# Moving the state's products, K's decays and the old state's decay to the front of a step in a linear-attention and feed-forward kernel

## The chip, the cores and the metric

The kernel runs on one core of a Trainium2 chip. The metric is the device time of one execution in microseconds, lower is better. Three runs of the kernel before took 573.32, 575.26 and 572.74 us, median 573.32.

The engines are named as in the profile: PE multiplies matrices (PEld is its weight load), DVE is the vector engine, ACT the scalar engine, POOL the GpSimd engine, and SP issues most DMAs.

## The reference

An attention block with a decaying state (RWKV-6) for 4 batches, 8 heads, 768 tokens and 48 channels a head, followed by a feed-forward block with a gated activation over the 3072 tokens:

```python
def _attn_ref(r, k, v, w, u):
    state = np.zeros((B, H, D, D))
    for t in range(S):
        cur = np.einsum('bhd,bhe->bhde', u[None] * kt, vt)
        y[:, :, t] = np.einsum('bhd,bhde->bhe', rt, state + cur)
        state = wt[:, :, :, None] * state + np.einsum('bhd,bhe->bhde', kt, vt)

def _moe_ref(x, w_in, w_out):                  # (3072, 384) (384, 2048) (2048, 384)
    h = x @ w_in
    sp = np.maximum(h, 0.0) + np.log1p(np.exp(-np.abs(h)))
    return (h * erf(sp)) @ w_out
```

All data is float32.

## The kernel before

**Tiles and steps.** The work is cut into 12 steps (`n_steps`): step s handles 128 tokens of two batches, with all heads, and the two pairs of batches alternate, so step s continues the state that step s - 2 left. A step's 128 tokens are two halves of 64 (`NC = 2`). The attention of a step does this:

- `prepare(s)`, a generator, runs a step ahead, in portions that a `next(following, None)` or a token `F` sends off. For the late steps it has POOL multiply the decays into totals (`tot_sb`, L438), and then DVE and POOL work out the terms inside blocks of 16 tokens side by side: products of r and k with `u` (L565, L568), of k and r within a block (`multiply`, L515 to L525, and `multiply_last`, L534), decays applied to r and k (`fade`, L493), decays combined (L486), and sums over the channels (`sum_up`, L559). It sends k, by now multiplied with its decays inside the block, through DRAM into the layout that the state needs (`kTs[s]`, DMAs L607 and L617), and the sums the same way (L609, L611).
- `level_products` (L671) multiplies r and k for spans of 32 and of 64 tokens; `take_level` puts them into `own`, by a masked copy on DVE (L681) or a copy on ACT (L688).
- `from_own` (L703) multiplies `own` with v into `y`, in two halves, `swap` 1 and 0, with a small copy on DVE between them (`fence`, L712); `through_state` (L729) adds what the old state and the state in the middle of the step (`middle`) give, copies `y` to `xT` and sends some of it on by DMAs. In the late steps the `y` of step s - 1 is made at the front of step s.
- `state_part` (L778) multiplies k with v for both halves. From them come `middle` (old state decayed, plus the first half; L857) and the new state (`middle` decayed, plus the second half; L863). The decays are multiplied in by POOL (L832, L860) into the tile `faded`. K is first multiplied with the decays over blocks (`spread[s]`, L837, on DVE).

The feed-forward block runs beside it on PE: `hidden` (L1153) multiplies `xT` of step s - 1 with `w_in` in eight pieces, each into one of two tiles `m` in PSUM and copied out by ACT (L1162); softplus and erf follow on ACT (L1109, L1113), the gating multiplication on DVE (L1118). `project_fast` (L1275) multiplies the gated result of step s - 3 with `w_out` in seven pieces; sums of blocks (`blend`, L1252 to L1258, on DVE) and copies into lanes of PSUM (`to_lane`, L1233, on ACT) save one of eight products. It takes the two tiles `m` as well: the first is last read by DVE at L1295, the second at L1300, and the first two pieces of `hidden` behind it go into the same two tiles.

**Order.** Every engine works through its instructions in the order in which the code issues them. For steps five to eleven that order is written out in `attend_late`, which calls `run` at seven places (`front`, `near`, 0 to 4); each place has a list of tokens: `P` is a piece of `project_fast`, `H` a piece of `hidden`, `s`, `e` and `m` softplus, erf and gating of a chunk, `k` a copy to a lane, `S` a blend, `F` a portion of `prepare`:

```python
USUAL = (
    "s P", "m", "ey P m s P P ep P", "m k22y P F P k11p F F", "S1", "S2 S3 H k12y S4 H F",
    "s H ey m H H F s H ep H H",
)
```

The products for 32 tokens, for 64 tokens and for the state use the same bank of PSUM, one after the other (`products(..., 0)`); the other bank is a lane. SP's queue has, at place 3, the loads of rows and decays of later steps. In step eleven there are no pieces of `hidden` behind the state's products; the weights are combined there on DVE (L1330), and after it the hidden products of the last two steps are made together.

Of the kernel before, what the change touches and what calls it, by code (L numbers as in the profile page):

```python
# [17 lines left out]
P = 128  # L18
# [3 lines left out]
HC = 64  # L22
NC = 2
# [17 lines left out]
DIRECT = 4  # L41
NEAR_LOG = 4
# [49 lines left out]
def kernel(  # L92
# [14 lines left out]
    nc = tc.nc  # L107
    PSUM = bass.MemoryType.PSUM

    n_steps, _, _, JP, C = rkw.shape  # L110
    NH, D = v.shape[2:]
    NP = JP // NJ
    NE = NH // JP
# [5 lines left out]
    SPC = NB // NJ  # L119
# [20 lines left out]
    middle = const.tile([P, JP, D], FP32, name="middle")  # L140
    faded = [const.tile([P, JP, D], FP32, name="faded")] * NC
# [22 lines left out]
    def products(shape, n=None):  # L164

        if n is None:
            n = turns["next"]
            turns["next"] = 1 - n
        names = "abc"[: len(shape) - 1]
        return banks[n][:].rearrange(  # L170
            f"p ({' '.join(names)}) -> p {' '.join(names)}", **dict(zip(names, shape[1:]))
        )

    loaded = {}
# [8 lines left out]
    def load_w(s):  # L183
        ws[s] = ins.tile([P, JP, C], FP32, name="w")
        nc.sync.dma_start(out=ws[s][:], in_=rkw[s][:, 2])
# [52 lines left out]
    def near_log(s):  # L238
        return NEAR_LOG - (s == DIRECT)
# [97 lines left out]
    def rows(e, n=D):  # L337
        return slice(e * EP, e * EP + n)

    both = slice(0, EP + D)  # L340
# [49 lines left out]
    def prepare(s):  # L390


        in_t = loaded[s][0]
        if s < DIRECT:
            rk1 = att.tile([P, 2, JP, C], FP32, name="rk1", bufs=1)
            ready[s] = (rk1,)
            parts = 1 if s else NJ
            def multiply_u(i, x):
                n = slice(i * JP // parts, (i + 1) * JP // parts)
                with_u, plain = (  # L400
                    [
                        t.rearrange("p n (t two) -> p n t two", two=2)[..., one]
                        for t in (rk1[:, x, n], in_t[:, x, n] if s else turns["first"][:, i, x])
                    ]
                    for one in (x, 1 - x)
                )
                if not s and not (x and not i):
                    nc.vector.tensor_mul(
                        with_u[0], with_u[1],
                        u_sb[:, :, None].to_broadcast([P, NP, C // 2]),  # L410
                    )
                    nc.vector.tensor_copy(out=plain[0], in_=plain[1])
                    return
                for p in range(NP):
                    of = slice(p, None, NP)
                    nc.scalar.mul(
                        out=with_u[0][:, of], in_=with_u[1][:, of], mul=u_sb[:, p : p + 1]
                    )
                nc.scalar.copy(plain[0], plain[1])

            if s < 2:
                for i in range(parts):
                    for x in range(2):
                        multiply_u(i, x)
                return
            yield
            yield
            multiply_u(0, 0)
# [42 lines left out]
        levels = near_log(s)  # L471
# [16 lines left out]
        def fade(engine, x, level):  # L488

            half = 1 << level - 1  # L490
            of = split(totals[level - 1], 1)[1 if x is k else 0][:, :, 0]
            to = split(x, half)[0 if x is k else 1]
            engine.tensor_mul(  # L493
                to, to, of[:, :, None, :].to_broadcast([P, NEAR // 2 // half, half, D])
            )
# [71 lines left out]
        fade(beside, k, 1)  # L567
        nc.vector.tensor_mul(own_terms, own_terms, r)  # L568
        fade(nc.vector, r, 1)
        if levels < NEAR_LOG:  # L570
            yield
        sum_up(1)
        multiply(nc.vector, 2)
# [67 lines left out]
    kTs, spread = {}, {}  # L641

    def parts_of(s):

        c, i = divmod(s, SPC)
        in_t, vt = loaded[s]
        made, tots, tot = ready[s]
        ends = tot.rearrange("p (n h) -> p n h", h=NC)
        return c, in_t, vt, made, states[i][c % 2], states[i][1 - c % 2], ends

    def by_pair(t):

        return lambda x, n: t[:, x, n]
# [40 lines left out]
    def from_own(s, own, swap):  # L694
        vt = loaded[s][1]
        for j in range(NJ):
            for q in range(0, NP, 2):
                for h in range(NC):
                    e = h ^ swap
                    for p in (q, q + 1):  # L700
                        n = j * NP + p
                        t = slice(h * HC, (h + 1) * HC)
                        nc.tensor.matmul(  # L703
                            y[at(e, p), e, p // 2, j, t],
                            lhsT=vt[t, n * NE + e, :], rhs=own[t, e * JP + n, :],
                            start=swap == 1 and not j and not q, stop=True,
                            skip_group_check=True,
                        )

    def fence():  # L710

        nc.vector.tensor_copy(  # L712
            out=seen[:].rearrange("p (e g t) -> p e g t", e=NE, g=NP),
            in_=y[:].rearrange("p e q j t -> p e (q j) t")[..., HC - 1 : HC + 1],
        )
# [53 lines left out]
    def state_part(s, kT, ps, halves=None):  # L769

        vt = loaded[s][1]
        if halves is None:
            halves = range(1 if s >= n_steps - SPC else NC)
        for n in range(JP):
            for h in halves:
                for e in range(NE):
                    t = slice(h * HC, (h + 1) * HC)
                    nc.tensor.matmul(  # L778
                        ps[h][e][rows(e), n, :D],
                        lhsT=kT[t, e * JP + n, :],  # L780
                        rhs=vt[t, n * NE + e, :],
                        start=True,
                        stop=True,
                    )
# [27 lines left out]
    def attend_late(s, run):  # L812

        c, in_t, vt, own, S, S_next, ends = parts_of(s)
        RK = by_pair(in_t)
        before = s - 1 if s - 1 > DIRECT else None
        if before:
            from_own(before, ready[before][0], 1)
            fence()
        pp = products([P, NE, JP, HC], 0)  # L820
        level_products(pp, RK, LOG - 1)
        scale(s, LOG - 1)
        take_level(own, pp, LOG - 1)
        run("front", None)
        if before:
            from_own(before, ready[before][0], 0)
            through_state(before, xTs[before])
            if s + 1 < n_steps:
                load_step(s + 1)
        following = prepare(s + 1) if s + 1 < n_steps else iter(())  # L830
        next(following, None)
        nc.gpsimd.tensor_mul(faded[0][:], S[:], ends[:, :, 0:1].to_broadcast([P, JP, D]))  # L832
        next(following, None)
        run("near", None)
        next(following, None)
        kT = kTs[s]
        nc.vector.tensor_mul(  # L837
            kT[:].rearrange("p (e n) d -> p n e d", e=NE),
            kT[:].rearrange("p (e n) d -> p n e d", e=NE), spread[s][:],
        )  # L840
        run(0, following)

        pp = products([P, NE, JP, HC], 0)
        level_products(pp, RK, LOG)
        if s + 1 < n_steps:
            spread_blocks(s + 1, pp)
        take_level(own, pp, LOG)
        if s > DIRECT + 1:
            scale(s, LOG)
        run(1, following)  # L850
        if s == DIRECT + 1:
            scale(s, LOG)
        ps = products([P, NC, JP, HC], 0)
        ps = [[ps[:, h]] * NE for h in range(NC)]
        state_part(s, kT, ps)
        run(2, following)
        nc.vector.tensor_add(middle[both], faded[0][both], ps[0][0][both, :, :D])  # L857
        run(3, following)
        if s < n_steps - SPC:
            nc.gpsimd.tensor_mul(  # L860
                faded[1][:], middle[:], ends[:, :, 1:2].to_broadcast([P, JP, D])
            )
            nc.vector.tensor_add(S_next[both], faded[1][both], ps[1][0][both, :, :D])  # L863
        run(4, following)

    def attend_first(xT):
# [590 lines left out]
        run_late(s, order[k])  # L1457


    STAGES_LATE = ("front", "near", 0, 1, 2, 3, 4)  # L1460
    LATE = {
        DIRECT + 1: (
# [73 lines left out]
    for kk in range(KT):  # L1536
        n = D // KT
        to, of = (x.rearrange("p (e m) -> p e m", e=NE) for x in (apart[:, kk], ident[:]))
        nc.vector.tensor_copy(out=to[:, :, D:], in_=of[:, :, kk * n : (kk + 1) * n])
    load_first()  # L1540
    with tc.manual_schedule(
# [15 lines left out]
        for s in range(n_steps):  # L1557
# [44 lines left out]
            def run(n, following):  # L1602
                if n == 3 and s < n_steps - 2:
                    load_rows(s + 2)
                if n == 3 and s + 3 < n_steps:
                    load_w(s + 3)
                run_late(s, LATE.get(s, USUAL)[STAGES_LATE.index(n)], following)

# [11 lines left out]
        s = n_steps  # L1620
# [107 lines left out]
```

## Time and profile before

| | |
|---|---|
| median of three runs | 573.32 us (572.74 to 575.26) |
| profiled execution, its own time | 574.36 us |
| its span | 572.6 us |
| PE busy | 564.2 us (99%), 7320 instructions |
| DVE busy | 452.7 us (79%), 506 |
| ACT busy | 358.5 us (63%), 495 |
| POOL busy | 246.8 us (43%), 265 |
| granted clock of PE | 0.999 |
| state products L778 | 205 ns each in the median, 704 records |
| hidden products L1153, 128x256 | 382 ns each, 960 records |

A row of the view by time reads: start, duration, engine, line, operation, tile written and tiles read, shapes, count, and in brackets how long the engine stood idle before and what released it. A matmul of float32 leaves two records and they are pipelined, so the start of the next group says more than a group's own duration. The spans on POOL are rough. In the view by stretches each row gives the length of the stretch and the busy time of each engine in it.

Step seven runs from 276.99 us to 321.29 us, counted from the first `y` product at its front.

### The profile page before, as it was taken

The numbers are of one execution on the slowest core, as the hardware profiler recorded it, in microseconds if no ns is written. First come the engines' busy times: TensorE is split into PE (matmuls) and PEld (weight loads), VectorE is DVE, ScalarE is ACT, GpSimd is POOL, SyncE is SP. The second block draws the span as 40 slices with busy tenths as digits, with TensorE's granted clock in tenths as the row PEclk, the third lists the DMA queues.
The fourth block names the chain that finished last, engine by engine and source line by source line (L and its number), as shares of the span: only waits on it lengthen the run. The fifth ranks groups of instructions, "written<-read, shape, count | busy, mean of one in ns | idle before, by whom it ended". The sixth has DMA issues, their size and how long they took to land.

```text
span 572.6 us, 16719 instructions
## 1 busy us (share of the span) xinstructions
PE 564.2 (99%) x7320; PEld 500.6 (87%) x7320; DVE 452.7 (79%) x506; ACT 358.5 (63%) x495; POOL 246.8 (43%) x265
## 2 busy tenths in 40 slices
PE   8899999999999999999999999999999999999997
PEld 5688887578998998998998998898898899989997
DVE  8774886999899899799699599599599596477730
ACT  3658877645458858747756766766675771489500
POOL 4557380731885884384285185176075000000000
PEclk9999999999999999999999999999999999999999
DMA  7596671440426324245245236234232201000000
GB/s 256 199 297 269 224 224 43 187 158 10 148 64 188 104 63 163 38 158 168 35 145 176 40 121 198 41 112 166 47 112 84 47 9 35 2 2 1 27 29 27
DMA packets 54082, 63.24 MB, mean 110 GB/s; under 512 B 35161, under 2 KB 40569, under 8 KB 52985
## 3 DMA queue, kind: packets, MB, share of 16 engines
q1 hardware_dynamic: 53624, 61.98, 34.4%
q8 instruction: 57, 0.93, 0.7%
q10 hardware_dynamic: 384, 0.20, 0.1%
q14 instruction: 17, 0.13, 0.1%
HBM read 52.39 MB, written 8.69 MB: 107 GB/s over the span
## 4 chain that ended last, share of the span: by engine, by line
PE 89%; DVE 5%; DMA 2%; ACT 1%; POOL 1%; issue 1%; SPq 0%; DVEq 0%; ACTq 0%; POOLq 0%
PE m L1275 33%; PE m L1153 32%; PE c L1378 6%; PE pp L671 5%; PE m L1185 4%; PE y L703 2%; PE y L729 2%; PE pp L778 2%; DVE in L364 1%; DMA words<-in_moe_w_in 1%; PE pp L990 1%; PE pp L1063 1%; DMA u_sb<-in_u 1%; DVE h L1118 1%; POOL tot_sb L386 0%
## 5 line engine op out<-in xcount | busy, mean ns | idle before, releaser
L1153 PE MATMUL m<-xT,w_in_sb 128*128 128x256 f32 x960 | 214.9, 382 | 0.2 <-ACT h L1162 0.2
L1153 PEld LDWEIGHTS m<-xT,w_in_sb 128*128 128x128 f32 x960 | 179.9, 190 | 25.5 <-ACT h L1162 0.6
L364 DVE TENSOR_TENSOR in<-in,tot_sb 128x1024 f32<-128x1024 f32 (+1 forms) x55 | 77.4, 1408 | 5.9 <-PE pp L671 3.4
L1162 ACT COPY h<-m 128x512 f32<-128x512 f32 x80 | 46.3, 580 | 47.8 <-PE m L1153 47.5
L1275 PE MATMUL m<-mixed,h 128*128 128x192 f32 x320 | 56.7, 331 | 0.0
L1275 PE MATMUL m<-w_out_sb,h 128*128 128x192 f32 x320 | 56.2, 329 | 0.0
L1275 PEld LDWEIGHTS m<-mixed,h 128*128 128x128 f32 x320 | 51.8, 190 | 0.9
L1275 PEld LDWEIGHTS m<-w_out_sb,h 128*128 128x128 f32 x320 | 52.0, 190 | 0.5
L1275 PE MATMUL m<-w_out_sb,room 128*128 128x192 f32 x288 | 49.7, 326 | 0.0
L1275 PEld LDWEIGHTS m<-w_out_sb,room 128*128 128x128 f32 x288 | 47.3, 190 | 0.1
L1113 ACT ACT_TABLE_LOAD x28 | 35.9, 1283 | 10.5 <-DVE h L1118 8.4
L534 POOL TENSOR_TENSOR words<-words 128x384 f32<-128x384 f32 x28 | 39.7, 1448 | 0.0
L671 PEld LDWEIGHTS pp<-in 48*48 48x48 f32 (+4 forms) x2368 | 30.1, 120 | 10.9 <-issue 5.8
L493 POOL TENSOR_TENSOR words<-words,own 128x384 f32<-128x384 f32 x21 | 30.1, 1433 | 22.0 <-DVE words L524 13.0
L1109 ACT ACT_TABLE_LOAD x28 | 35.9, 1283 | 1.8 <-issue 1.3
L486 POOL TENSOR_TENSOR own<-rest 128x384 f32<-128x384 f32 x7 | 9.7, 1384 | 61.0 <-ACT o L1281 61.0
L671 PE MATMUL pp<-in 48*48 48x32 f32 (+4 forms) x2368 | 34.0, 206 | 0.3 <-DVE in L364 0.3
L534 POOL TENSOR_TENSOR rk<-words 128x384 f32<-128x384 f32 x28 | 33.4, 1225 | 0.0
L559 DVE TENSOR_REDUCE sums<-rk 128x16 f32<-128x768 f32 (+2 forms) x31 | 31.6, 1021 | 0.0
L438 POOL TENSOR_TENSOR tot_sb<-tot_sb 128x256 f32<-128x256 f32 (+4 forms) x50 | 29.9, 598 | 3.8
L1109 ACT ACTIVATE room<-h 128x1024 f32<-128x1024 f32 x28 | 29.6, 1057 | 0.3
L319 POOL TENSOR_TENSOR w_out_sb<-w_out_sb,rest 128x768 int32<-128x768 int32 x8 | 18.3, 2290 | 21.9 <-DVE w_out_sb L311 21.9
(214 smaller groups left out, 1008.7 us busy)
## 6 DMA issues: line engine op xcount, KB each, us to landing
in<-in_rkw SPq DMA_DIRECT2D x8, 1024.0 KB, 5.3
words<-in_moe_w_in SPq DMA_DIRECT2D x16, 384.0 KB, 6.3
words<-in_moe_w_out SPq DMA_DIRECT2D x16, 384.0 KB, 4.4
words<-in_rk_rows SPq DMA_DIRECT2D x8, 768.0 KB, 6.4
w<-in_rkw SPq DMA_DIRECT2D x11, 512.0 KB
v<-in_v SPq DMA_DIRECT2D x12, 384.0 KB, 5.7
out<-o SPq DMA_DIRECT2D x23, 192.0 KB, 3.0
in<-in_rkw SPq DMA_DIRECT2D x7, 512.0 KB, 5.9
```

The source lines that it names most:

```text
L364: nc.vector.tensor_mul(halves, halves, view(tots[level - 1], 0, [[1, n], [2, nb], [0, half]]))
L438: nc.gpsimd.tensor_mul(new, pair[:, :, 0], pair[:, :, 1])
L493: engine.tensor_mul(to, to, of[:, :, None, :].to_broadcast([P, NEAR // 2 // half, half, D]))
L534: engine.tensor_mul(to[:, i], r[:, half:], k[:, part * rows + i, None].to_broadcast([P, half, D]),)
L559: nc.vector.tensor_reduce(out=to, in_=of, axis=mybir.AxisListType.X, op=ALU.add)
L671: nc.tensor.matmul(to, lhsT=rk(1, n)[rows(e), s0 : s0 + m], rhs=right, start=True, stop=True,)
L1109: nc.scalar.activation(sp_room, chunks[0], AF.Softplus)
L1113: nc.scalar.activation(at, sp_room, AF.Erf)
L1153: nc.tensor.matmul(ps[:, ff, :], lhsT=w_in_sb[:, g * FG + f + ff, kk * P : (kk + 1) * P], rhs=xT[:, kk, :], start=kk == 0, stop=kk == KT - 1,)
L1162: nc.scalar.copy(h[:, f : f + FT, :], ps[:])
L1275: nc.tensor.matmul(to, lhsT=a[:, f], rhs=b[:, f], start=start and f == 0, stop=f == FG - 1, skip_group_check=True,)
L1378: nc.tensor.matmul(to[:, f], lhsT=turns["weights"][b][:, i * FT + f], rhs=turns["tokens"][a], start=a + b in STARTS and not f, stop=True, ...
```

## The change

It concerns steps seven to eleven (`JOINED`). At the front of such a step, ahead of everything else, K is multiplied with its decays on DVE (`fade_k`), the old state with its decay on POOL (`fade_state(0, S)`), and the first portion of `prepare(s + 1)`, the totals on POOL, is sent off. Directly behind `through_state` of the step before, PE makes the state's products, DVE adds `middle`, POOL multiplies it with its decay, the second portion of `prepare` begins, and DVE adds the new state. In `prepare` a further `yield` behind the second decay of r (L569) splits that portion, so that the new state's addition comes between. All other steps keep their order. The same instructions are issued on every engine, and the order of SP's DMAs does not change. On POOL the old state's decay now stands ahead of the totals of the next step, and the decay of `middle` ahead of the first combined decay of `prepare` (L486).

```diff
@@ prepare
-        in_t = loaded[s][0]
         if s < DIRECT:
+            in_t = loaded[s][0]
...
         fade(nc.vector, r, 1)
-        if levels < NEAR_LOG:
+        if levels < NEAR_LOG or s > DIRECT + 2:
             yield
         sum_up(1)
@@ -814,6 +814,37 @@
         c, in_t, vt, own, S, S_next, ends = parts_of(s)
         RK = by_pair(in_t)
         before = s - 1 if s - 1 > DIRECT else None
+        joined = s in JOINED
+        following = prepare(s + 1) if s + 1 < n_steps else iter(())
+        kT = kTs[s]
+
+        def fade_state(h, of):
+            nc.gpsimd.tensor_mul(
+                faded[h][:], of[:], ends[:, :, h : h + 1].to_broadcast([P, JP, D])
+            )
+
+        def fade_k():
+            nc.vector.tensor_mul(
+                kT[:].rearrange("p (e n) d -> p n e d", e=NE),
+                kT[:].rearrange("p (e n) d -> p n e d", e=NE), spread[s][:],
+            )
+
+        def state_products():
+            ps = products([P, NC, JP, HC], 0)
+            state_part(s, kT, [[ps[:, h]] * NE for h in range(NC)])
+            return ps
+
+        def next_middle(ps):
+            nc.vector.tensor_add(middle[both], faded[0][both], ps[both, 0, :, :D])
+
+        def next_state(ps):
+            if s < n_steps - SPC:
+                nc.vector.tensor_add(S_next[both], faded[1][both], ps[both, 1, :, :D])
+
+        if joined:
+            fade_k()
+            fade_state(0, S)
+            next(following, None)
         if before:
             from_own(before, ready[before][0], 1)
             fence()
@@ -827,17 +858,23 @@
             through_state(before, xTs[before])
             if s + 1 < n_steps:
                 load_step(s + 1)
-        following = prepare(s + 1) if s + 1 < n_steps else iter(())
-        next(following, None)
-        nc.gpsimd.tensor_mul(faded[0][:], S[:], ends[:, :, 0:1].to_broadcast([P, JP, D]))
+        if joined:
+            ps = state_products()
+            next_middle(ps)
+            if s < n_steps - SPC:
+                fade_state(1, middle)
+            next(following, None)
+            next_state(ps)
+        else:
+            next(following, None)
+            fade_state(0, S)
+            if before:
+                next(following, None)
         next(following, None)
         run("near", None)
         next(following, None)
-        kT = kTs[s]
-        nc.vector.tensor_mul(
-            kT[:].rearrange("p (e n) d -> p n e d", e=NE),
-            kT[:].rearrange("p (e n) d -> p n e d", e=NE), spread[s][:],
-        )
+        if not joined:
+            fade_k()
         run(0, following)
 
         pp = products([P, NE, JP, HC], 0)
@@ -850,17 +887,15 @@
         run(1, following)
         if s == DIRECT + 1:
             scale(s, LOG)
-        ps = products([P, NC, JP, HC], 0)
-        ps = [[ps[:, h]] * NE for h in range(NC)]
-        state_part(s, kT, ps)
+        if not joined:
+            ps = state_products()
         run(2, following)
-        nc.vector.tensor_add(middle[both], faded[0][both], ps[0][0][both, :, :D])
+        if not joined:
+            next_middle(ps)
         run(3, following)
-        if s < n_steps - SPC:
-            nc.gpsimd.tensor_mul(
-                faded[1][:], middle[:], ends[:, :, 1:2].to_broadcast([P, JP, D])
-            )
-            nc.vector.tensor_add(S_next[both], faded[1][both], ps[1][0][both, :, :D])
+        if not joined:
+            fade_state(1, middle)
+            next_state(ps)
         run(4, following)
 
     def attend_first(xT):
@@ -1457,6 +1492,7 @@
         run_late(s, order[k])
 
 
+    JOINED = set(range(DIRECT + 3, n_steps))
     STAGES_LATE = ("front", "near", 0, 1, 2, 3, 4)
     LATE = {
         DIRECT + 1: (
```

## The prediction

> **What bounds the kernel now.** I read the busy times of each step first (one stretch per step, from the start of the `y` products of one step to the next), then the instructions of step seven in order of time.
>
> ```profile
> core 0: us, PE busy (x) PEld busy (x) DVE busy (x) ACT busy (x) POOL busy (x), PEclk, DMA share, GB/s
> 276.99:321.29 44.30, 44.30 (x533) 40.60 (x533) 37.41 (x38) 29.24 (x37) 22.93 (x26) 1.00 0.39 117
> 409.89:454.18 44.29, 44.29 (x502) 40.59 (x501) 36.94 (x37) 29.24 (x37) 18.79 (x16) 1.00 0.28 78
> 454.18:498.50 44.32, 44.32 (x633) 42.10 (x633) 30.99 (x49) 21.33 (x34) 0.00 (x0) 1.00 0.05 15
> ```
>
> Steps seven to ten take 44.30 us each and PE is busy all of it at full clock; DVE works 37.4, POOL 22.9. PE is the bound, so there is no wait of PE in these steps to take away. What can change is a wait that appears, or the few tenths PE loses where products change shape. These rows of step seven fix the places (PE, then DVE, POOL, ACT):
>
> ```profile
> 282.02 0.63 PE L729 MATMUL y<-in,middle 48*48 48x64 f32 x32
> 282.58 2.87 PE L1275 MATMUL m<-mixed,h 128*128 128x192 f32 x16
> 285.28 2.76 PE L1275 MATMUL m<-w_out_sb,room 128*128 128x192 f32 x16
> 296.81 2.76 PE L1275 MATMUL m<-w_out_sb,h 128*128 128x192 f32 x16
> 299.51 0.94 PE L778 MATMUL pp<-v,kT 64*48 64x48 f32 x64
> 300.37 20.99 PE L1153 MATMUL m<-xT,w_in_sb 128*128 128x256 f32 x96
> ...
> 280.19 0.94 DVE L565 TENSOR_TENSOR rk<-words,u_row 128x768 f32<-128x768 f32 x1
> 282.51 1.24 DVE L493 TENSOR_TENSOR words<-words,rest 128x384 f32<-128x384 f32 x1
> 293.58 1.33 DVE L837 TENSOR_TENSOR kT<-kT,spread 128x768 f32<-128x768 f32 x1
> 298.34 0.54 DVE L1295 TENSOR_TENSOR o<-o,m 128x384 f32<-128x384 f32 x1
> 304.00 1.21 DVE L1252 TENSOR_TENSOR room<-h,y 128x1024 f32<-128x1024 f32 x1
> 305.13 0.54 DVE L857 TENSOR_TENSOR middle<-faded,pp 112x384 f32<-112x384 f32 x1
> ...
> 281.92 1.41 POOL L486 TENSOR_TENSOR own<-rest 128x384 f32<-128x384 f32 x1 [12.45 <-ACT o L1281]
> 283.29 1.31 POOL L493 TENSOR_TENSOR words<-words,rest 128x384 f32<-128x384 f32 x1
> 305.75 0.83 POOL L860 TENSOR_TENSOR faded<-middle,tot_sb 128x384 f32<-128x384 f32 x1 [2.76 <-DVE middle L857]
> ...
> 305.24 1.02 ACT L1233 COPY y<-h 128x1024 f32<-128x1024 f32 x1 [1.39 <-DVE room L1252]
> 311.88 0.58 ACT L1162 COPY h<-m 128x512 f32<-128x512 f32 x1
> ```
>
> To see: from 280.19 to 315 DVE runs practically without a pause, so whatever holds it at the front of the step reaches everything behind. Two of those things are what PE waits for. The hidden products (L1153) come in eight pieces of 20.92/8 = 2.615 us and take turns in the two `m` tiles. The first piece needs the tile that DVE's L1295 reads until 298.88; it starts at 300.37, so the slack is 1.49. The sixth piece starts at 300.37 + 5 x 2.615 = 313.45 and needs ACT's fourth copy (L1162), over at 312.46: slack 0.99. That copy stands behind ACT's copy to a lane at 305.24, which waited for DVE's L1252 and follows it 0.03 us after its end.
>
> **The change, part by part.** No instruction is added or removed on any engine; three groups move.
>
> *K times decays* (DVE, 768 elements) goes from between the fourth and fifth multiplication behind the products to the front, ahead of the copy that fences `y`. There DVE stands idle: in step seven it ends L633 at 274.25 and waits 3.46 us until 277.72. K is loaded by a DMA issued at 270.30, 4.6 us to landing by the listing of DMAs, so 274.9; the multiplication ends at about 276. Its `spread` was issued one step earlier, at 252 by the same 44.3 us rhythm, and is long there. Cost 0. Behind it queue the fence and L364; PE needs the fence only at 281.09, so K could land 3 us later before PE noticed. From its old place 1.26 us of DVE disappear (293.58 to 294.84).
>
> *State products* (PE, 0.86 us from start to start) go from 299.51 to 282.58. PE's total is unchanged, less one change of shape: a piece of 16 instructions of L1275 takes 2.70 next to small products (282.58 to 285.28) and 2.60 away from them, so about 0.10 a step in PE's favour.
>
> *The two additions that take these products* (`middle` L857, and the new state L863, 0.54 each, 0.46 from start to start) and POOL's multiplication between them (0.83) go along. This is the part that costs. `middle` now stands directly behind the masked copy that ends at 280.3, but its products end at 282.5 + 0.94, about 283.45. DVE stands still for over three microseconds; with 0.07 from PE's end to DVE's start (277.65 to 277.72 at the fence) and 0.46 for itself, L565 starts at 283.95 instead of 280.19: **3.75 us late**. Behind it queue all of the next step's preparation and, after that, the gating multiplications (L1118), L1295, L1300, L1252.
>
> What then adds and subtracts: POOL's first instruction of the preparation (L486) stood at 281.92; now POOL does the state's 0.83 first, which needs `middle`. DVE and POOL take turns wherever both read from SBUF: L493 on DVE takes 1.24 beside POOL against 0.56 for the same size in quieter places, K's multiplication 1.33 here and 0.95 in step eleven, where POOL is idle. Followed turn by turn (L565, POOL's 0.83, L515, POOL's L486 of about 0.87, L568, POOL's L493 of about 0.87, DVE's L493, the new state, the sum), the stretch from L565 to L518 takes 6.2 instead of 4.6 us: 1.6 more, with two more turns of POOL between DVE's. Lowest value 0: the new state's 0.46 fits into the 0.43 that L518 waits for POOL anyway. I take 1.6, because the same turns give every duration of the present rows to about 0.1. Next, K's 1.26 are gone, and DVE's L364 of 512 elements (1.31 here, 0.69 in step eleven) then falls between two of POOL's turns: minus 0.6 at most, nothing at least. I take 0.6. So L1295 and L1252 are late by 3.75 + 1.6 - 1.26 - 0.6 = **3.5 us**; from both ends 2.0 (without the turns, with the 0.6) to 4.1.
>
> The stall follows: the first hidden piece waits for L1295 until 302.4, some 2.1 us. The fourth copy of ACT ends at 312.46 + 3.5 = 315.96; the sixth piece starts at 316.03 instead of 313.45. **Steps seven, eight and nine are 2.6 us longer each** (between 2.0 - 0.99 + 0.07 = 1.1 and 3.2). It does not build up: each step DVE is set again by PE's state products, and at the next front L633 keeps about 2 us to the `y` products (now 2.8), because `middle` and the state no longer stand late in the step.
>
> [...]
>
> Step ten has no POOL multiplication and no new state (the last two steps need none), so POOL's L486 runs in DVE's pause: 3.75 late, less 0.6 for turns that are saved, 1.26 and 0.6, leaves about 1.3 at L1252, a stall of 1.3 - 0.99 + 0.07 = 0.4; with the lost turns it could be 1.3, and nothing at the other end. Step eleven has no hidden pieces behind its state products. Its L1295 would end at 474.86 + 3.75 - 0.87 = 477.74, where PE's next product into that tile starts at 477.75: 0 to 0.2.
>
> **Sum**: 3 x 2.6 + 0.4 + 0.1 = 8.3. The profiled execution took 574.36 (its span 572.6 and 1.76 around it), so it would take 582.7; the median of the three runs is 1.04 lower, so 573.32 + 8.3 = **581.6**. By the ends of the terms: 3 x 1.1 to 3 x 3.2 and 0 to 1.5, so 576.6 to 584.4.
>
> **Rivals.**
> *POOL's turns cost nothing.* L518 is only 3.8 late (the state's 0.46 goes into the wait of 0.43), L364 keeps its 1.31, L1252 is 2.55 late: 1.63 a step, about 0.2 in step ten and eleven; 573.32 + 5.1 = 578.4. For it: POOL starts with DVE idle and may slip in between reductions, which are not slowed (0.54, 0.95). Against it: 1.24 against 0.56. Chance 0.2.
> *The delay is absorbed and PE gains from the shapes.* One mechanism, at PE's change from small to full products: 0.10 us, perhaps 0.2 with the start of the hidden products, in five steps; 573.32 - 0.5 to - 1.0, so 572.6. It decides when L1252 comes less than 0.9 late, L1295 less than 1.4. For it: DVE is idle 6.7 us of each step. Against it: that idle time lies at the end and the front of a step, behind L1252. Chance 0.12.
> *K comes late at the front.* If its DMA landed 5 us later than now, the fence would hold PE as well; per microsecond beyond that five of total, so 587 with one. For it: its issue moves back with DVE's sums, by some 3 us against a step 2.6 longer. Against it: that leaves 3 us. Chance 0.05.
> That the change might not act is excluded: steps seven to eleven have their products behind `y` in the instruction order.
>
> **How the numbers follow.** The forecast has 0.63, so 581.6; the range 576.5 to 584.5 takes in its terms and the first rival, and leaves out the second and third, 0.17. A measurement of this kernel can tell about 0.5% (2.9 us) from no change. Slower by more: forecast, first and third rival, 0.88; within: most of the second, 0.10; faster: 0.02, as nothing here is worth 2.9 us.
>
> **What would show it.** Right: a gap of about 2 us of PE ahead of the first hidden product in steps seven to nine, released by DVE's L1295 (L1330 in the changed file), a smaller gap before the fifth or sixth, released by ACT; DVE idle for 3.2 us ahead of `middle`; steps of some 46.9 us, step ten near 44.7. The turns: DVE's L515 and L568 longer than 0.55 and 0.95. Wrong: PE still dense and steps of 44.2 (the second rival), steps of 45.9 with short DVE rows (the first), or the fence waiting for K with PE idle ahead of the second half of `y` (the third).

## The result, and the profile after

The changed kernel takes 581.07 us in the median of six runs (579.98 to 581.71), the kernel before beside it 573.25: a ratio of 1.0128 (95% interval 1.011 to 1.0146), 7.8 us slower, where 8.3 were forecast. The profiled execution has a span of 579.9 us against 572.6. The view by stretches, one stretch for each step from its first `y` product (length; busy time of each engine; granted clock), shows where they are:

```profile
core 0: us, PE busy (x) PEld busy (x) DVE busy (x) ACT busy (x) POOL busy (x), PEclk, DMA share, GB/s
277.24:323.65 46.41, 44.86 (x533) 40.28 (x532) 36.75 (x38) 29.37 (x37) 24.64 (x26) 1.00 0.37 112
416.47:461.53 45.06, 44.84 (x501) 40.27 (x500) 36.36 (x37) 29.37 (x37) 18.99 (x16) 1.00 0.28 77
461.53:484.51 22.98, 22.98 (x402) 22.17 (x401) 18.18 (x26) 13.80 (x19) 0.00 (x0) 1.00 0.03 6
```

Step seven is 2.11 us longer than the 44.30 before, and eight and nine have the same 46.41. Step ten is 0.77 longer than its 44.29 before. Step eleven, up to the first `y` product behind its last piece of `project_fast`, takes 22.98 where the kernel before took 23.02:

```profile
454.18:477.20 23.02, 23.02 (x403) 22.19 (x406) 19.71 (x29) 13.79 (x19) 0.00 (x0) 1.00 0.05 15
```

That is 3 x 2.11 + 0.77 - 0.04 = 7.06 of the 7.3 us between the spans; another 0.25 was there at the front of step seven already, in steps that did not change. The clock is full in steps seven to eleven, and in seven to ten PE is no longer dense. Step seven by time (PE, DVE, POOL, ACT; start, duration, line, count, and in brackets the idle time before and its releaser):

```profile
282.72 0.90 PE L778 MATMUL pp<-v,kT 64*48 64x48 f32 x64
283.55 2.87 PE L1310 MATMUL m<-mixed,h 128*128 128x192 f32 x16
302.10 21.63 PE L1188 MATMUL m<-xT,w_in_sb 128*128 128x256 f32 x96 [1.55 <-DVE o L1330]
...
275.24 0.96 DVE L827 TENSOR_TENSOR kT<-kT,spread 128x768 f32<-128x768 f32 x1 [0.74 <-DMA kT<-k_blocks]
277.98 0.17 DVE L712 COPY seen<-y 128x16 f32<-128x16 f32 x1 [1.77 <-PE y L703]
283.76 0.56 DVE L838 TENSOR_TENSOR middle<-faded,pp 112x384 f32<-112x384 f32 x1 [3.21 <-PE pp L778]
284.23 0.95 DVE L565 TENSOR_TENSOR rk<-words,u_row 128x768 f32<-128x768 f32 x1
285.10 0.55 DVE L515 TENSOR_TENSOR rk<-words 128x384 f32<-128x384 f32 x1
285.57 0.95 DVE L568 TENSOR_TENSOR rk<-rk,words 128x768 f32<-128x768 f32 x1
286.55 1.07 DVE L493 TENSOR_TENSOR words<-words,rest 128x384 f32<-128x384 f32 x1
289.47 1.03 DVE L518 TENSOR_TENSOR rk<-words 128x384 f32<-128x384 f32 x2 [0.92 <-POOL words L493]
299.55 0.90 DVE L364 TENSOR_TENSOR in<-in,tot_sb 128x512 f32<-128x512 f32 x1
301.50 0.54 DVE L1330 TENSOR_TENSOR o<-o,m 128x384 f32<-128x384 f32 x1
307.17 1.21 DVE L1287 TENSOR_TENSOR room<-h,y 128x1024 f32<-128x1024 f32 x1
...
284.39 2.81 POOL L822 TENSOR_TENSOR faded<-middle,tot_sb 128x384 f32<-128x384 f32 x1 [9.32 <-DVE middle L838]
287.17 1.31 POOL L486 TENSOR_TENSOR own<-rest 128x384 f32<-128x384 f32 x1
...
308.40 1.02 ACT L1268 COPY y<-h 128x1024 f32<-128x1024 f32 x1 [2.83 <-DVE room L1287]
```

The lines behind the changed part have moved: L1330 was L1295, L1287 was L1252, L1188 was L1153. DVE stands still for 3.21 us ahead of `middle`. Measured from the front of the step, which begins 0.25 later, L565 is 3.79 us late, L518 4.58, L1330 2.91 and L1287 2.92. PE waits 1.55 us ahead of the hidden products, until L1330 has freed their tile, and the eight pieces then take 21.63 us, where 20.88 is their length without a wait (below). K's multiplication at the front waits 0.74 us for its DMA and is over at 276.20, 1.8 us ahead of the fence.

### The profile page after: what moved, and what is told of

Same layout as the page of the kernel before. It is cut to its first block, busy times and chain, and to the rows that moved or that the text cites. A ratio compares the mean times of both kernels' runs of the same rounds, so it can differ in the third digit from the quotient of the medians.

```text
span 579.9 us, 16716 instructions
## 1 busy us (share of the span) xinstructions
PE 567.0 (98%) x7320; PEld 499.8 (86%) x7320; DVE 451.1 (78%) x506; ACT 359.0 (62%) x495; POOL 253.5 (44%) x265
## 4 chain that ended last, share of the span: by engine, by line
PE 61%; DVE 14%; issue 13%; POOL 10%; ACT 1%; POOLq 0%; DVEq 0%; ACTq 0%
PE m L1188 23%; PE m L1310 17%; PE c L1413 6%; PE pp L671 5%; PE m L1220 4%; POOL words L493 3%; DVE h L1153 2%; DVE in L364 2%; DVE sums L559 2%; POOL words L534 2%; DVE words L524 2%; POOL tot_sb L438 2%; PE y L703 1%; POOL rk L534 1%; PE m L1016 1%
## 5 line engine op out<-in xcount | busy, mean ns | idle before, releaser
L1188 PE MATMUL m<-xT,w_in_sb 128*128 128x256 f32 x960 | 217.6, 383 | 5.2 <-DVE o L1330 4.9
L1188 PEld LDWEIGHTS m<-xT,w_in_sb 128*128 128x128 f32 x960 | 178.8, 190 | 35.1 <-DVE o L1330 6.1
L364 DVE TENSOR_TENSOR in<-in,tot_sb 128x1024 f32<-128x1024 f32 (+1 forms) x55 | 76.9, 1398 | 7.1 <-PE pp L671 4.5
L534 POOL TENSOR_TENSOR words<-words 128x384 f32<-128x384 f32 x28 | 43.6, 1586 | 0.0
L493 POOL TENSOR_TENSOR words<-words,own 128x384 f32<-128x384 f32 x21 | 30.1, 1435 | 22.8 <-DVE words L524 13.0
L822 POOL TENSOR_TENSOR faded<-middle,tot_sb 128x384 f32<-128x384 f32 x5 | 10.1, 2023 | 51.5 <-DVE middle L838 51.5
L559 DVE TENSOR_REDUCE sums<-rk 128x16 f32<-128x768 f32 (+2 forms) x31 | 31.7, 1022 | 0.0
L534 POOL TENSOR_TENSOR rk<-words 128x384 f32<-128x384 f32 x28 | 30.6, 1122 | 0.0
```

What stands on the lines that cost most here:

```text
L364: nc.vector.tensor_mul(halves, halves, view(tots[level - 1], 0, [[1, n], [2, nb], [0, half]]))
L493: engine.tensor_mul(to, to, of[:, :, None, :].to_broadcast([P, NEAR // 2 // half, half, D]))
L534: engine.tensor_mul(to[:, i], r[:, half:], k[:, part * rows + i, None].to_broadcast([P, half, D]),)
L559: nc.vector.tensor_reduce(out=to, in_=of, axis=mybir.AxisListType.X, op=ALU.add)
L1188: nc.tensor.matmul(ps[:, ff, :], lhsT=w_in_sb[:, g * FG + f + ff, kk * P : (kk + 1) * P], rhs=xT[:, kk, :], start=kk == 0, stop=kk == KT - 1,)
```

## The experiments

The line numbers of the runs are those of their own files; the tiles tell which is which. The code excerpts leave out lines at `...`. Each run was timed beside the kernel before on its chip.

**The front alone.** K's decays, the old state's decay and the totals at the front, everything else where it was:

```diff
         if joined:
             fade_k()
             fade_state(0, S)
             next(following, None)
...
-        if joined:
-            ps = state_products()
-            next_middle(ps)
...
+        ps = state_products()
         run(2, following)
+        next_middle(ps)
```

> Only K's decays and the old state's decay (with the totals of the next step) stand at the front of steps seven to eleven; the state's products and their two additions stay where they were before the change. Theory (DVE's pause ahead of the addition to middle is the whole cost): without that pause nothing waits, 573.2 us like the kernel before, within 1 us. Rival (the front is the cost: K's DMA or POOL's totals come too late there): most of the 7.8 us remains, 578 or more.

574.53 us, ratio 1.0019 (0.9998 to 1.004); steps seven to ten take 44.29 to 44.30. The front costs nothing there.

**Both additions later.** The products stay early, the additions and POOL's multiplication go where their operands are ready:

```diff
             ps = state_products()
+            next(following, None)
             next_middle(ps)
             if s < n_steps - SPC:
                 fade_state(1, middle)
             next(following, None)
             next_state(ps)
...
-        if s == DIRECT + 1:
+        if s == DIRECT + 1 or s > DIRECT + 2:
             yield
         multiply(nc.vector, 3)
...
```

> As the changed kernel, but DVE adds middle only behind the decay of r (L493), POOL multiplies it behind its first decay of k, and DVE adds the new state two portions later, ahead of the products of level three. PE's order is that of the changed kernel. Theory (the pause): no DVE pause, L1330's place no later than before, PE dense; 573.25 less five changes of shape of 0.10 us, 572.7 us. Rival one (taking turns with POOL's multiplication costs as much as the pause): half of it or more remains, 577 or more. Rival two (the early products themselves disturb PE): 580.

572.81 us, ratio 0.9983 (0.997 to 0.9996): slightly faster than the kernel before, with PE's order as in the changed kernel. Step seven by stretches:

```profile
276.77:320.72 43.95, 43.95 (x533) 40.58 (x532) 37.31 (x38) 29.35 (x37) 23.07 (x26) 1.00 0.40 118
```

And its timeline, PE and DVE:

```profile
282.25 0.90 PE L778 MATMUL pp<-v,kT 64*48 64x48 f32 x64
283.07 2.87 PE L1312 MATMUL m<-mixed,h 128*128 128x192 f32 x16
299.91 20.88 PE L1190 MATMUL m<-xT,w_in_sb 128*128 128x256 f32 x96
...
283.46 0.54 DVE L838 TENSOR_TENSOR middle<-faded,pp 112x384 f32<-112x384 f32 x1
```

PE is dense and the step 0.35 us shorter than before. The parts can be read off: about 0.11 less from `y` to the state's products and 0.04 less for these, 0.10 less for the last piece of `project_fast` ahead of the hidden products (2.60, 297.31 to 299.91, for 2.70), 0.11 less for the hidden products (20.88 for 20.99). `middle` has no idle time before it. So the pause and the link through POOL, which this run takes away together, were the whole loss, and the early products are a small gain.

**The first tile sooner.** One question was which of the two waits sets the step. Place 1 had `"m k22y P F P k11p F F"`; here a piece of `project_fast` stands ahead of the gating multiplication:

```diff
+    SOONER = list(USUAL)
+    SOONER[3] = "P m k22y F P k11p F F"
+    LATE.update({n: SOONER for n in range(DIRECT + 3, n_steps - 1)})
```

> As the changed kernel, but in steps seven to ten L1330, which frees the first tile m, stands one gating multiplication (1.13 us) sooner on DVE. Theory (two waits in a row, and the later one, ACT's copies behind the first blend, sets the step): the first gap of PE shrinks from 1.55 to about 0.5 us and the hidden products behind it get longer by as much; 581 us, within 0.7. Rival (the tile of L1330 sets it): three steps shorter by 1.1 us each, 577.6 us.

580.77 us, ratio 1.0116 (1.0094 to 1.0137), and the step is 46.41 long, as in the changed kernel:

```profile
300.67 8.34 PE L1188 MATMUL m<-xT,w_in_sb 128*128 128x256 f32 x36 [0.41 <-DVE o L1330]
309.69 13.73 PE L1188 MATMUL m<-xT,w_in_sb 128*128 128x256 f32 x60 [0.69 <-ACT h L1197]
```

The first gap went from 1.55 to 0.41, and a gap of 0.69 came behind the third piece, released by ACT's copies, with some tenths more inside the rows. The time PE does not lose at L1330 it loses behind ACT: the first blend (L1287) and the copies behind it set the step.

**A pause by itself.** The kernel before, with memsets of 192 elements on DVE at the place of the pause, in steps seven to ten, and nothing moved; first 18 of them, then 9, 3, 12 and 15:

```diff
         take_level(own, pp, LOG - 1)
+        if DIRECT + 2 < s < n_steps - 1:
+            for _ in range(18):
+                nc.vector.memset(idle[:], 0.0)
         run("front", None)
```

> The kernel before with 18 small memsets (192 elements) on DVE behind the masked copy of steps seven to ten, some 3 us in which DVE does nothing of use; nothing else moves. Theory (PE's slack against L1252 is 0.99 less 0.07 us): each of the four steps is longer by the pause less 0.92, about 2 us; 573.25 + 8.3 = 581.5 us. Rival (the pause does not matter, the moved products do): 573.2 us.

597.18 us, ratio 1.0397 (1.0374 to 1.042): a miss, for two reasons. A memset took 0.32 us and not the 0.17 that I had read from another small instruction, so the pause was 5.7 us; and the granted clock fell to 0.50 behind PE's gaps, 2.32 us in step seven (last section). Smaller pauses followed:

> As the run with 18 memsets, with 9 of them (0.32 us each there, so a pause of 2.9 us, near the 3.2 us that DVE stands still in the changed kernel). Of a pause DVE makes good about 0.58 us before the first blend. Theory: L1252's place 2.3 us late, less the slack of 0.92: each of steps seven to ten 1.4 us longer, 5.5 us in all (ratio 1.0096); PE's gaps stay under 2 us and its clock full. Rival (the 18 memsets cost so much only through the halved clock that they brought, and a short pause costs nothing): ratio 1.000.

> The same with 3 memsets, a pause of 0.96 us. Theory (a slack that has to be used up first): L1252's place 0.4 us late, inside the slack of 0.92, ratio 1.000 within 0.002. Rival (every microsecond of DVE counts): 3 to 4 us, ratio 1.006.

Nine memsets: ratio 1.0095 (1.0071 to 1.0119), a step of 45.71, clock full. Three: 1.0023 (1.0005 to 1.004), a step of 44.59 where none was expected to be longer: the pause of 0.8 us grew to 1.09 at the first blend instead of shrinking, because the multiplication that is L568 in the kernel before took 1.76 us instead of 0.95 (last section). What counts is how late that blend comes, not how long the pause is.

**POOL's link later, the pause kept.** The further `yield` is that of the run with both additions later:

```diff
             next_middle(ps)
+            next(following, None)
             if s < n_steps - SPC:
                 fade_state(1, middle)
             next(following, None)
             next_state(ps)
...
```

> As the changed kernel with DVE's pause ahead of middle kept, but POOL's multiplication of middle stands behind its first decay of k, and the new state's addition two portions later, as in the run that added both later. Theory (pause plus turns with POOL): POOL's first instruction of the preparation runs in DVE's pause again, L518 3.3 instead of 4.6 us late, steps seven to nine 1.2 instead of 2.1 us longer, step ten as before; 4.4 us in all, ratio 1.0077. Rival one (the pause alone): ratio 1.0125, as the changed kernel. Rival two (POOL's link alone): 0.998, as with both additions later.

578.75 us, ratio 1.0083 (1.0053 to 1.0112), and a step of 45.28: 0.98 longer than before, where the changed kernel is 2.11 longer.

```profile
275.51:320.79 45.28, 44.86 (x534) 40.28 (x533) 36.56 (x38) 29.37 (x37) 23.35 (x26) 1.00 0.38 114
```

The pause, with POOL's first decay (L486) running inside it, costs about one microsecond a step. The other 1.13 us go with POOL's multiplication of `middle` in the chain and the addition of the new state, which this run moves together and does not tell apart.

**Step six too.**

> The run with both additions later, extended to step six. Theory (each step whose state products stand behind y is 0.35 us shorter by fewer changes of shape on PE, as steps seven to eleven were in that run): 6 x 0.35 = 2.1 us less than before, ratio 0.9963, span some 570.5 us. Rival (the 0.35 came from something particular to those steps): no more than with five steps.

572.23 us, ratio 0.997 (0.995 to 0.999), span 570.4; step six takes 44.11 instead of 44.30, 0.19 us less where 0.35 had been expected. In this step K's load lands later: K's multiplication ends 2.58 us behind the front (in step seven of the changed kernel 1.04 us ahead of it), DVE's work behind it waits, and the first blend is 0.61 us late. The run is faster than the kernel before; against the run with steps seven to eleven (0.9983) the intervals overlap, so the sixth step's share is seen in the trace only.

**Two more pauses**, one run each, to see where the clock falls:

> The pause of 12 memsets, 3.8 us. Five kinds of step so far (1.09, 1.56, 1.78, 2.21 and 2.92 us late at the first blend) were longer by their lateness less 0.80. Theory: 3.1 to 3.2 us late, each of the four steps 2.3 to 2.4 us longer, span some 582; PE's gap ahead of the hidden products 1.7 us as in the changed kernel, its clock full. Rival (the clock halves from any gap that is longer than the changed kernel's on): more than 3 us a step.

> The pause of 15 memsets, 4.7 us. With the clock full: 4.1 us late, each of four steps 3.3 us longer, span some 586. If PE's gaps (2.0 us or more ahead of the hidden products and some tenths ahead of the state's products) already halve the clock as with 18 memsets: 5 us and more a step, span 592 or more.

Spans of 582.9 and 589.0 us, where 582 and, with a full clock, 586 were expected; the clock fell in one step of the first run and in three of the second (last section). The steps that kept the full clock are 46.69 and 47.65 long. Put together, first blend late against its place in the kernel before (27.01 us behind the front), and the step longer than its 44.30 (step ten: 44.29):

| step of | first blend late, us | step longer, us | difference |
|---|---|---|---|
| from six on, step six | 0.61 | -0.19 | 0.80 |
| 3 memsets | 1.09 | 0.29 | 0.80 |
| changed kernel, step ten | 1.56 | 0.77 | 0.79 |
| POOL's link later | 1.78 | 0.98 | 0.80 |
| 9 memsets | 2.21 | 1.41 | 0.80 |
| changed kernel, step seven | 2.92 | 2.11 | 0.81 |
| 12 memsets | 3.19 | 2.39 | 0.80 |
| 15 memsets, step nine | 4.15 | 3.35 | 0.80 |

Whatever delays the first blend, by 0.61 to 4.15 us here, the step is longer by that delay less 0.80 us. That is the slack of the chain from the blend over ACT's copies to the hidden pieces. The first row says what the early products are worth: by 0.80 - 0.35, their 0.35 us stay whole only while the blend is less than 0.45 us late.

## Why the prediction was right, point by point

- **The pause.** L565 was put at 3.75 us late and is 3.79 late. DVE's idle time is 3.21 us, forecast 3.2. That the early products with late additions lose nothing, and a pause by itself does, shows the cause.
- **Turns with POOL, put at 1.6 us: too much.** From L565 to L518 the stretch took 4.45 us (the prediction reads 4.6) and takes 5.24, so 0.79 more: 0.46 for the addition of the new state and 0.49 for a longer wait for POOL's L493, less 0.16 at L493 on DVE. The prediction had POOL come in between L565 and L515, and again ahead of L568; L515 and L568 kept their 0.55 and 0.95. Instead POOL's multiplication, 0.83 alone, lasted 2.81: it came to its end only when DVE's L493, 0.03 us behind L568, left the first gap. That the two hold each other up these rows show: POOL's 2.81 us, and 1.07 for DVE's L493 behind them, which took 0.56 at 290.53, where it began ahead of POOL's. "Wherever both read from SBUF", as the prediction has it, no run shows: in the kernel before the sum L559 kept its 0.54 us at 283.67, beside POOL's L493 (283.29 to 284.60), and here the row of instructions on DVE kept POOL out. Which of the two goes first at the seams I had assumed, and wrongly. The rival that turns cost nothing is refuted: it put L518 at 3.8 us late and a step at 1.63, and they are 4.58 and 2.11; the run with POOL's link later, whose step is 1.13 us shorter, agrees.
- **K's 1.26 and L364.** K's term was as forecast. L364 came out at 0.90 from 1.31, 0.41 less instead of 0.6. So 3.79 + 0.79 - 1.26 - 0.41 = 2.91 us late at L1330 and L1287, against 3.5 forecast. (The low end of that term, 2.0, should have been 1.9 by its own numbers, 3.75 - 1.26 - 0.6.)
- **The stall.** Forecast 2.6 a step from 3.5 us late and a slack of 0.99 less 0.07; measured 2.11 from 2.91 and 0.80. The slack was 0.12 smaller than read, because the prediction held the end of ACT's fourth copy against the sixth piece's first product, at 313.45. The piece's first weight load waits for that copy already, and in the kernel before it starts at 313.21; with 0.05 us from the copy's end to the load, as at 315.69 in the changed kernel, that leaves 0.70. The other tenth is regained in the piece: when it had to wait, its second product starts 0.32 us behind the load, and 0.43 in the row without a wait. The order of the two waits was right: the tile first, ACT's copies deciding.
- **Step ten** was put at 0.4 and took 0.77: its first blend was 1.56 us late, not 1.3, and the slack was smaller. **Step eleven** lost nothing.
- **The shapes.** 0.10 to 0.2 a step had been granted to PE; it is 0.35, seen only where no wait swallows it. The second rival, 0.5 to 1.0 us faster, fits the version that does not pause (ratio 0.9983, about 1.0 us).
- **K late at the front** did not happen: DVE waited 0.5 to 0.8 us for the DMA, ahead of a fence that was not yet due. In step six of the wider run K did hold up the fence, to 2.50 us behind the front, but PE's second half of `y` stood at its usual 4.10.

In a step of seven to nine two errors went against each other: a delay 0.59 too long made the stall too large, a slack 0.12 too wide (0.80 for 0.92) made it too small, which leaves the 0.5 between 2.6 and 2.11. That they partly cancel is luck. Over the steps the sum is 7.06 where 8.3 was forecast, and step ten's 0.37 more gives back a part of it. The medians lie nearer, 7.8 and 8.3, because 0.25 at the front of step seven and some tenths between runs, which no term of the forecast stood for, came on top.

## What to carry to other kernels

Moving a product earlier on the busy engine is not free when its consumer is moved along to a place in another engine's order where the product is not ready yet: everything queued behind the consumer inherits the wait (here 3.21 us of DVE ahead of `middle`, and a step 2.11 us longer). Move the products, and let the consumer stand where its operand has just arrived. For each engine that is not the bound, look up which of its instructions frees a buffer of the one that is, and how much later it may come; here 37 of 44 us busy left room for 0.8 us at one place.

## What had not been expected of the hardware

**PE's clock fell behind gaps of 1.7 to 2.3 us, and not behind all of them.** With 15 memsets PE stands still for 2.3 us ahead of the hidden products in each of four steps, and for 0.27 us ahead of the state's products. The view by stretches, steps seven to ten:

```profile
275.70:324.42 48.72, 46.13 (x533) 41.77 (x532) 40.49 (x53) 29.24 (x37) 22.87 (x26) 0.96 0.36 106
324.42:373.11 48.69, 46.11 (x534) 41.81 (x533) 40.49 (x53) 29.24 (x37) 22.87 (x26) 0.96 0.36 106
373.11:420.76 47.65, 45.06 (x533) 40.34 (x532) 40.50 (x53) 29.25 (x37) 22.87 (x26) 1.00 0.34 98
420.76:470.76 50.00, 47.40 (x502) 42.72 (x501) 40.12 (x52) 29.31 (x37) 18.71 (x16) 0.93 0.24 69
```

Around the hidden products of step ten, in finer stretches:

```profile
446.80:449.00 2.20, 2.13 (x5) 1.77 (x6) 2.20 (x4) 1.55 (x2) 2.17 (x2) 0.50 0.64 202
449.00:451.00 2.00, 2.00 (x6) 1.56 (x6) 1.97 (x2) 0.00 (x0) 1.86 (x1) 0.50 0.30 104
451.00:453.00 2.00, 2.00 (x7) 1.60 (x6) 2.00 (x2) 0.58 (x1) 0.00 (x0) 0.52 0.50 197
453.00:455.00 2.00, 2.00 (x11) 1.77 (x10) 2.00 (x4) 1.02 (x1) 0.83 (x1) 1.00 0.00 0
```

The granted clock (third number from the end) is 0.50 for some six microseconds in step ten, comes back earlier in steps seven and eight, and stays full in step nine after the same gap. Each drop costs 1.0 to 2.4 us on top of the gap. With 18 memsets, gaps of 2.32 us and of 1.25 ahead of the state's products in step seven, the clock fell as well: 0.93, 0.97 and 0.97 in the mean of three stretches of 51 us from the front of that step on. With 12 memsets and gaps of 1.69 to 1.70 us, step ten alone lost about a microsecond in the same way against the 46.69 of the other three:

```profile
416.88:464.62 47.74, 46.04 (x501) 41.76 (x501) 39.37 (x49) 29.24 (x37) 18.74 (x16) 0.96 0.26 73
```

The changed kernel's 1.55 us lost none in its profile, 1.00 in each of steps seven to ten. Equal gaps fared differently: of four of 2.31 to 2.33 us, with 15 memsets, three were followed by a drop; of four of 1.69 to 1.70, with 12, one. What decides it was not tried.

**A row of vector instructions kept POOL out for longer than one instruction.** POOL's 0.83 us (L860 in the kernel before) took 2.81 to 2.82 behind three of DVE that followed each other without a gap, L565, L515 and L568, in each of steps seven to nine. With three memsets the third of the same three took longer instead:

```profile
284.80 1.76 DVE L569 TENSOR_TENSOR rk<-rk,words 128x768 f32<-128x768 f32 x1
```

This is L568 of the kernel before, 0.95 us there. The 0.81 us more are near the 0.83 that POOL's L860 takes in the kernel before; from these two numbers I estimate that here POOL's first decay came in between the second and the third, and the third had to wait. That the gap of 0.03 us ahead of L493 let POOL in is read from the times alone, and what decides which of the two goes first at such a seam stays open.
